# Where group 0's q and k are cut in two: strips 4 + 3 and 3 + 4, or 5 + 2 and 2 + 5

## The chip, the core and the metric

One NeuronCore of a Trainium2 chip runs the whole program. The metric is the device time of one execution in microseconds (us). The profile comes from one execution; its span is some 1.8 us shorter than the device time of the same execution (387.1 against 388.88 us for the kernel before). Engine names are those of the profile: PE is TensorE's matrix products, PEld its weight loads, DVE is VectorE, ACT is ScalarE, POOL is GpSimd, SP the sync engine. SP, ACT and POOL each issue DMA transfers from a queue of their own. "Group 0" is the first four heads of the first batch entry; a group has 7 strips of 64 tokens.

## The reference

Sigmoid attention over 8 batch entries, 12 heads, 448 tokens and head size 64, then a two-layer network with the tanh form of GELU over the 3584 tokens.

```python
scores = scale * np.matmul(q, k.transpose(0, 1, 3, 2)) - np.log(S)
attn = 1.0 / (1.0 + np.exp(-scores))
attn_out = np.matmul(attn, v)                     # (8, 12, 448, 64)
x = attn_out.transpose(0, 2, 1, 3).reshape(B * S, H * D)
h = x @ w_in                                      # 768 -> 2048
g = 0.5 * h * (1.0 + np.tanh(c * (h + 0.044715 * h * h * h)))
return g @ w_out                                  # 2048 -> 768
```

## The kernel before

The kernel plans itself at build time: operations with dependencies and modelled costs go into a list scheduler, which fixes the order of every engine. On the chip each engine then executes its list in that order and waits on semaphores.

Group 0 is special: its k and q are loaded, cast to bf16, transposed on TensorE and copied out of PSUM in two parts each, so that the first scores can start early.

```python
CUTS = {"q": ((0, NJ // 2 + 1), (NJ // 2 + 1, NJ)), "k": ((0, 3), (3, NJ))}     # NJ = 7: q 4 + 3, k 3 + 4
...
if g == 0:
    for x, (lo, hi) in enumerate(CUTS[nm]):
        both = [plan.add(Op("ld%s0.%d.%d" % (nm, x, c), eng, ... dma_start(d[:, c:c + w, lo * D:hi * D], ...),
                 ..., pkt=(8 * w, FIRST * (hi - lo) / NJ)))        # modelled packets
                for (eng, c, w) in (("AQ" if (nm, x) == ("q", 0) else "SP", 0, 2),)]
...
# group 1: q on ACT's queue after the warm-up activation, k on SP's
ld[g] = plan.add(Op(..., "AQ" if (nm, g) == ("q", 1) else "SP", ..., ([warm1] if (nm, g) == ("q", 1) else []) + ...))
...
# the first v load, on GpSimd's queue, waits for k's first part
deps = later(av, g - NVB) + (ld_k[(0, 0)].ops if g == 0 else [])
...
# part casts: modelled cost by strips; k's second part waits for the copy of q's second
who = "ACT" if (nm, x) == ("q", 1) else "DVE"
... (hi - lo) * (107.0 if who == "ACT" else 75.0) + 60.0, ...
...
def qk_needs(g, j):            # what a strip's scores wait for
    if g:
        return [tr_q.get(g), tr_k.get(g)]
    return [tr_q.get((0, 0)), tr_q.get((0, 1)), tr_k.get((0, 0 if j < CUTS["k"][0][1] else 1))]
...
plan.run()                     # fixes the orders
waits, level = emit(plan, None, None)
```

## Time and profile before

| | kernel before |
|---|---|
| device time, first three runs | 389.72 us median (389.63 to 389.81) |
| span of the profiled execution | 387.1 us |
| PE busy | 382.0 us (99%), from 40 to 380 us 339.95 of 340.00 |
| ACT | five sigmoids from 7.43 us, 0.23 us idle, sixteen from 11.82; second table load at 25.11 |
| chain that ended last | opens with the load of group 1's q, issued 2.81, landed 9.47 |

Read it from the end: TensorE has no room after some 30 us, so only the start can move the time, and in the start the question is which wait ends last. The prediction shows the lines.

### The profile page before, as it was taken

The page shows a single profiled execution, that of the slowest core. Times are in us where ns is not written, and L with a number is a line of the kernel's source. Part 1 is how long each engine was busy: PE and PEld are TensorE (multiplying, and loading weights), DVE is VectorE, ACT ScalarE, POOL GpSimd, SP SyncE. Part 2 cuts the span into 40 slices and gives each one's busy share as a digit, 9 for nine tenths or more (in the row PEclk, how much of TensorE's full clock was granted, in tenths as well). Part 3 has the DMA queues.
Part 4 walks back from the last instruction along what each step waited for, and adds up shares of the span by engine and source line. Part 5 has one row for each costly group of instructions (what it writes and reads, how often), then busy time and mean ns, then how long its engine had stood idle before and what let it go on. Part 6 is the DMA issues. An engine that isn't in the chain of part 4 may idle for free.

```text
span 387.1 us, 7517 instructions
## 1 busy us (share of the span) xinstructions
PE 382.0 (99%) x3218; PEld 203.7 (53%) x3218; DVE 155.8 (40%) x273; ACT 227.6 (59%) x337; POOL 53.1 (14%) x84
## 2 busy tenths in 40 slices
PE   8999999999999999999999999999999999999996
PEld 5434445555555555555555555554555555555565
DVE  3446733147680085702864057610767017400000
ACT  4999962268564575546755476635856467544221
POOL 5994110001110111001110011100201000000000
PEclk9999999999999999999999999999999999999999
DMA  8999999747885079903779048950779401110133
GB/s 226 186 203 203 209 206 321 121 88 182 186 194 103 8 171 210 233 5 109 147 204 204 4 120 203 204 99 0 185 185 215 82 0 42 43 41 2 41 83 81
DMA packets 64226, 51.74 MB, mean 134 GB/s; under 512 B 36289, under 2 KB 60737, under 8 KB 64193
## 3 DMA queue, kind: packets, MB, share of 16 engines
q1 hardware_dynamic: 48928, 36.81, 39.3%
q0 software_dynamic: 14560, 13.64, 22.4%
q10 hardware_dynamic: 704, 0.82, 0.6%
q8 instruction: 25, 0.41, 0.4%
q14 instruction: 9, 0.07, 0.0%
HBM read 45.61 MB, written 11.01 MB: 146 GB/s over the span
## 4 chain that ended last, share of the span: by engine, by line
PE 94%; ACT 3%; DMA 2%; DVE 1%; issue 0%; ACTq 0%
PE ps L824 39%; PE ps L779 36%; PE ps L632 9%; PE ps L680 7%; ACT at L643 2%; DMA qf<-in_q_dram 2%; PE ps L755 2%; PE ps L589 1%; ACT L377 0%; ACT th L652 0%; DVE qb L363 0%; DVE at L656 0%; DVE kb L363 0%; PE ps L586 0%; ACT xT L362 0%
## 5 line engine op out<-in xcount | busy, mean ns | idle before, releaser
L652 ACT ACTIVATE th<-ps 128x896 f32<-128x896 f32 x147 | 126.9, 928 | 45.2 <-PE ps L632 45.2
L824 PE MATMUL ps<-w_out,gT 128*128 128x384 bf16 (+2 forms) x912 | 152.9, 324 | 0.1
L779 PE MATMUL ps<-xT,w_in 128*128 128x448 bf16 x738 | 143.3, 353 | 0.0
L656 DVE TENSOR_SCALAR at<-th 128x896 bf16<-128x896 f32 x147 | 92.0, 626 | 127.3 <-ACT th L652 126.5
L824 PEld LDWEIGHTS ps<-w_out,gT 128*128 128x128 bf16 x912 | 85.9, 98 | 65.5 <-ACT th L652 5.9
L793 ACT ACTIVATE gT<-ps 128x448 bf16<-128x448 f32 x128 | 69.7, 549 | 79.2 <-PE ps L779 78.3
L779 PEld LDWEIGHTS ps<-xT,w_in 128*128 128x128 bf16 x738 | 71.4, 98 | 68.3 <-issue 3.1
L632 PE MATMUL ps<-qT,kT 64*64 64x448 bf16 x672 | 48.1, 358 | 0.3 <-ACT at L643 0.2
L512 POOL DMA_DIRECT2D vb<-in_v_dram x24 | 14.9, 620 | 237.7 <-PE ps L632 234.5
L680 PE MATMUL ps<-at,vb 64*64 64x448 bf16 x672 | 38.0, 350 | 0.1
L363 DVE COPY ob<-ps 128x384 f32<-128x384 f32 x43 | 23.9, 555 | 25.4 <-PE ps L824 24.3
L632 PEld LDWEIGHTS ps<-qT,kT 64*64 64x64 bf16 x672 | 15.7, 105 | 24.2 <-issue 9.8
L680 PEld LDWEIGHTS ps<-at,vb 64*64 64x64 bf16 x672 | 19.5, 107 | 12.1 <-issue 1.1
L362 ACT ACTIVATE ob<-ps 128x384 f32<-128x384 f32 (+2 forms) x14 | 6.6, 468 | 25.4 <-PE ps L824 25.4
L363 DVE CAST xT<-ps 128x448 bf16<-128x448 f32 x27 | 16.6, 623 | 11.0 <-PE ps L680 11.0
L514 POOL DMA_DIRECT2D vb<-in_v_dram x24 | 18.3, 762 | 0.2 <-issue 0.2
L643 ACT ACTIVATE at<-ps 128x896 bf16<-128x896 f32 x21 | 17.4, 924 | 0.7 <-PE ps L632 0.7
L363 DVE CAST kb<-kf 128x896 bf16<-128x896 f32 (+2 forms) x21 | 12.8, 610 | 11.0 <-DMA kf<-in_k_dram 10.5
L363 DVE CAST qb<-qf 128x896 bf16<-128x896 f32 (+1 forms) x20 | 12.3, 616 | 1.5 <-DMA qf<-in_q_dram 1.5
L362 ACT ACTIVATE xT<-ps 128x448 bf16<-128x448 f32 x21 | 11.6, 551 | 1.9 <-PE ps L680 1.9
L888 POOL DMA_DIRECT2D w_in<-in_moe_w_in_dram x16 | 10.2, 703 | 0.0
L436 PE MATMUL ps<-gT 128*128 128x128 bf16 (+1 forms) x54 | 6.9, 285 | 1.1 <-DVE gT L428 1.1
(31 smaller groups left out, 50.2 us busy)
## 6 DMA issues: line engine op xcount, KB each, us to landing
out_dram<-ob SPq DMA_DIRECT2D x54, 192.0 KB, 3.4
kf<-in_k_dram SPq DMA_DIRECT2D x19, 448.0 KB, 4.4
qf<-in_q_dram SPq DMA_DIRECT2D x18, 448.0 KB, 6.0
vb<-in_v_dram POOLq DMA_DIRECT2D x48, 112.0 KB, 5.4
w_out<-in_moe_w_out_dram POOLq DMA_DIRECT2D x4, 768.0 KB, 21.5
w_in<-in_moe_w_in_dram POOLq DMA_DIRECT2D x12, 192.0 KB, 11.6
kb<-in_k_dram POOLq DMA_DIRECT2D x4, 224.0 KB, 8.9
qb<-in_q_dram POOLq DMA_DIRECT2D x4, 224.0 KB, 9.3
```

Of the source, the lines that this page charges most:

```text
L362: return e.activation(o, i, AF.Copy)
L363: return e.tensor_copy(o, i)
L512: a = plan.add(Op("ldv%da" % g, "SWQ", lambda e, d=dst[0:64], ap=lo: e.dma_start(d, ap), deps, 610.0, 0.0, prio=order_v(g), sem="ldv%da" % ...
L514: c = plan.add(Op("ldv%db" % g, "SWQ", lambda e, d=dst[64:128], ap=hi: e.dma_start(d, ap), deps, 610.0, 0.0, prio=order_v(g), sem="ldv%db" ...
L632: r = mm(ps[64 * half:64 * half + 64, (x, y)[a], 0:S], kv[d, a, j, :], qv[d, a, :, :], start=True, stop=True)
L643: lambda e: e.activation(at[as_][:], both, AF.Sigmoid, bias=bias, scale=scale),
L652: lambda e: e.activation(th[ts][:], both, AF.Tanh, bias=0.5 * bias, scale=0.5 * scale),
L656: lambda e: e.tensor_scalar(at[as_][:], th[ts][:], 0.5, 0.5, op0=ALU.mult, op1=ALU.add),
L680: r = mm(ps[64 * c:64 * c + 64, banks[a], 0:S], vb[s][d, slot, j, :], at[as_][d, a, :], start=(j == 0), stop=(j == NJ - 1))
L779: r = mm(ps[:, bank, 0:S], w_in[:, kt, fc * 128:(fc + 1) * 128], xT[xb][:, kt, :], start=(kt == 0), stop=(kt == KT - 1))
L793: lambda e: e.activation(gT[:, fc, col:col + S], ps[:, bank, 0:S], AF.Gelu_apprx_tanh),
L824: r = mm(ps[:, bank, 0:hi - lo], gT[:, fc, col:col + 128], w_out[:, fc, lo:hi], start=(fc == 0), stop=(fc == FC - 1))
```

## The change

The intent: k's first part, on which the first scores wait, becomes smaller, so that 9 strips instead of 10 must land before the first scores. The price is a larger second part of k, on which the third strip's scores now wait too (before, only the fourth and later ones: `j < 3` above).

```diff
-        CUTS = {"q": ((0, NJ // 2 + 1), (NJ // 2 + 1, NJ)), "k": ((0, 3), (3, NJ))}
+        CUTS = {"q": ((0, 5), (5, NJ)), "k": ((0, 2), (2, NJ))}
```

This is the whole diff. The line reaches both the chip (sizes of loads, casts, transposes, copies) and the planner (their modelled costs).

## The prediction

> **What bounds the kernel now.** I read the page's busy shares first, then the chain that ended last in order of time, then the ACT timeline of the first 30 us, the waits there, and the DMA issues with their landing times. TensorE is busy 382.0 us of the 387.1 us span, and from 40 to 380 us it is busy 339.95 of 340.00 us. The change touches nothing there. It touches the first 9 us, so the question is how much later or earlier TensorE reaches its closed stretch. The chain tells what decides that:
>
> ```profile
> PE 382.0 (99%) x3218; PEld 203.7 (53%) x3218; DVE 155.8 (40%) x273; ACT 227.6 (59%) x337; POOL 53.1 (14%) x84
> ...
> 2.81 6.66 DMA qf<-in_q_dram
> 9.46 0.02 issue
> 9.48 0.76 DVE qb L363
> 10.24 0.60 DVE kb L363
> 10.85 0.04 issue
> 10.89 0.56 PE ps L586 x7
> 11.46 0.34 PE ps L632 x4
> 11.80 0.02 issue
> 11.82 3.35 ACT at L643 x4
> ```
>
> The columns are start, duration, engine and line. The transfer in the chain is 448 KB, issued at 2.81 us on ACT's queue: q of group 1, not of group 0. It lands at 9.47; VectorE casts q1, then k1 (k1 was issued at 2.26 and took 6.8, so it landed at 9.06 and waits for q1's cast in VectorE's fixed order); TensorE transposes k1, and only behind these seven transposes in its own fixed order come the scores of group 0's sixth strip, which start the sixth sigmoid at 11.82. From there ACT is closed:
>
> ```profile
> 7.43 4.15 ACT L643 ACTIVATE at<-ps 128x896 bf16<-128x896 f32 x5 [0.49 <-PE ps L632]
> 11.82 13.27 ACT L643 ACTIVATE at<-ps 128x896 bf16<-128x896 f32 x16 [0.23 <-PE ps L632]
> 25.11 1.28 ACT L648 ACT_TABLE_LOAD   x1
> ```
>
> Five sigmoids run from 7.43 to 11.58, ACT then idles 0.23 us, and sixteen run from 11.82 to 25.09 without a gap. All of group 0's own start (loads, casts, transposes, copies) lies before 7.43, its second part of k before 9. So group 0's path ends in **0.23 us of slack**.
>
> The loads concerned, with KB and us from issue to landing:
>
> ```profile
> kf<-in_k_dram SPq DMA_DIRECT2D x1, 448.0 KB, 6.8
> qf<-in_q_dram ACTq DMA_DIRECT2D x1, 448.0 KB, 6.7
> ...
> qf<-in_q_dram ACTq DMA_DIRECT2D x1, 256.0 KB, 4.0
> kf<-in_k_dram SPq DMA_DIRECT2D x1, 256.0 KB, 4.3
> kf<-in_k_dram SPq DMA_DIRECT2D x1, 192.0 KB, 3.6
> ...
> qf<-in_q_dram SPq DMA_DIRECT2D x1, 192.0 KB, 4.0
> ```
>
> A strip is 64 KB. With the issue times 0.74, 0.74, 1.26 and 1.75, the first part of k landed at 4.36, the first of q at 4.74, the second of q at 5.33 (ACT's cast starts there) and the second of k at 6.05.
>
> **What the Trainium skill says.** "DMA: Bandwidth & Descriptors", Issuing engines are not separate DMA queues: transfers issued from different engines run on the same 16 DMA engines and interleave. The trace agrees: in slices of 0.3 us from 3.0 to 5.4 us they move 346 to 392 GB/s, mean 371, at a busy digit of 9, though three queues issue. So what a load waits for is the bytes in front of it, whichever queue they are in. The same page, Specifications, puts the smallest transfer at full rate at 512 B; the new parts of two strips have rows of 2 x 64 x 4 = 512 B, just there, so I take no loss (no run yet shows it). "VectorE: DVE Perf Modes", The TRN2 errata: a fixed cost for each instruction plus cycles by size; at two elements a cycle and 0.96 GHz a strip of 128 elements adds 67 ns. The trace agrees: the cast of 384 columns took 360 ns, that of 512 took 427. "ScalarE: Activation LUTs", What ACT_TABLE_LOAD costs, gives one element a cycle at 1.2 GHz, 107 ns for a strip; the trace has ACT's cast of three strips at 523 ns and its copy at 491, and no second size to check the slope by.
>
> **The change part by part.** The number of instructions stays: two loads, two casts, two sets of transposes and two copies for q and for k, 14 transposes in all. Only sizes move.
>
> 1. Loads. Before the first score k's first part and all of q must land: 3 + 7 = 10 strips before, 2 + 7 = 9 after. One strip at 371 GB/s is 0.18 us, so q's second part should land near 5.15 instead of 5.33. The first parts of k and q together are seven strips in both kernels (3 + 4, 2 + 5), and so are the second parts; so q's first part, which is larger but shares with a smaller k, lands near 4.74 again, k's second part near 6.05, and q1 and k1 have the same bytes in front of them.
> 2. To the first score. VectorE casts q's five strips in 427 + 67 = 494 ns, from 4.76 to 5.25 (before: 5.19). TensorE starts q's transposes 0.17 us later, as before, 5.42; ACT's cast of two strips, 523 - 107 = 416 ns from 5.15, is done at 5.57, in time. Before, VectorE's copy of four strips began 0.77 us after the first of q's weight loads, ACT's of three strips 0.33 us after that, so 0.11 us for each transpose. After: VectorE's copy of five strips starts at 5.42 + 0.77 + 0.11 = 6.30 and takes 425 + 67 = 492 ns to 6.79; ACT's of two starts at 6.30 + 0.22 = 6.52 and takes 491 - 107 = 384 ns to 6.90. The old end was 6.95. So **the first score gains 0.05 us**, not the 0.18 us of the transfer, since the seven transposes start from VectorE's longer cast.
> 3. k's second part. Its cast waits for ACT's copy of q. The old path: cast 7.05 to 7.65 (600 ns), transposes, copy 8.14 to 8.56, third score at 8.54 (from the timeline). Five strips instead of four add about 0.08 (cast: 360 ns at three strips, 670 at seven, so 78 a strip) + 0.06 (a transpose; 7 took 0.56 - 0.16) + 0.07 (copy) = 0.21 us; less the 0.05 of step 2 the third score comes at 8.70. The third sigmoid started 9.04, some 0.43 after a score is enough, so 8.70 gives 9.13. **The third sigmoid is 0.09 us later than now.** It uses slack of 0.07 that was there and opens a hole of some 0.14 us against the second.
> 4. Groups 0's first five sigmoids thus end near 11.58 + 0.09 = 11.67. The sixth still waits for TensorE, 11.82. The slack falls from 0.23 to 0.14 us plus what the hole takes, and **nothing reaches the end**.
> 5. q1's landing. The v loads on GpSimd's queue wait for k's first part (wait of 3.2 us ended by kf). With two strips it may land 0.1 to 0.35 us sooner (nothing if the queues take turns row by row, two strips' worth of bytes if byte by byte: 128 KB at 371 GB/s). Then v enters the shared engines earlier and, with a third of them for 0.35 us, puts at most some 40 KB before q1: 0.1 us later. This part is on the path one for one. I take + 0.05.
>
> Sum: 0 from steps 1 to 4, + 0.05 from step 5: 389.72 + 0.05, say **389.8 us**.
>
> **The rivals.** (a) The early start reaches the end: if ACT were the chain from 7.43 on, the gain would be 0.05 to 0.18 us, 389.55 to 389.65. Against it speak the 0.23 us of idle and the chain, which passes through q1's load and not through group 0. (b) k's second part becomes the bound: the third score comes after its slot. If step 3 is short by 0.2 us, because VectorE's cast of five strips runs slower next to the descriptor writing of GpSimd (the cast of k's four strips took 600 ns, q's four 427), the hole exceeds the slack and 0.1 to 0.3 us reach the end: 389.8 to 390.0. (c) The order changes. The kernel's own planner at build time orders each engine's instructions by modelled times, in which the strip counts enter; shifted times can change the order of scores, transposes, first-layer parts and filler matmuls anywhere. For a small effect: the sums of strips are unchanged in each phase, so the planner's q1 and k1 hardly move, and the first score shifts by a little. For a large one: list scheduling at ties is jumpy. If k1's cast came ahead of q1's, it could start at 9.06 instead of 10.24, the sixth score would no longer wait and up to 0.23 us would be won, plus whatever follows. A bad reordering near 25 to 35 us, where ACT goes over to the other activation table and TensorE is not quite closed, could cost some tenths. A TensorE closed for 340 us leaves later orders little to lose: I give - 0.4 to + 0.8 us. (d) Row sizes of 512 B move slower than thought; both short parts are 256 KB in all, and even a halved rate costs 0.35 us in front of q1: 390.1.
>
> **Range and chances.** The three runs of before lie within 0.18 us. Steps 1 to 5 with (a), (b) and (d) cover 389.5 to 390.1; (c) widens it more to the slow side, since the old cut looks chosen by trial. I take 389.2 to 390.5. Two per cent are 7.8 us, which is more than everything before the first score can be worth (7.43 us of span), so: faster 0.01, same 0.98, slower 0.01.
>
> **What would show it.** In the changed profile the chain should still open with q of group 1 on ACT's queue, landing at 9.4 to 9.6 (step 5), with the sixth sigmoid near 11.8 to 11.9. The first sigmoid should start at 7.3 to 7.45 (step 2); ACT should show a small new hole before the third sigmoid (step 3); k's cast of 640 columns should take 0.65 to 0.7 us. The landings should be about 4.1 to 4.3, 4.7, 5.15 and 6.05 (step 1). I would be wrong if the chain went through group 0's load or through k's second part, if q1 landed away from 9.5 by more than 0.2 us, or if the order on VectorE around 9.5 to 11 us were another: then the reordering, and not the strips, made the time.

## The result

The changed kernel took 389.62 us (median of 6 runs, 389.31 to 390.03), the kernel before 389.53 us beside it (388.99 to 389.81). The ratio is 1.0005 with a 95% interval of 0.9992 to 1.0018: the same. A ratio here and below is the mean time of one kernel's fast runs over that of the other's of the same rounds, so not quite the ratio of the medians quoted.

All of the profile's totals stay: PE is busy 382.4 us of a span of 387.7. But the chain of waits does not open as before. From the chain that ended last of the changed kernel, in order of time (start, duration, engine and line):

```profile
8.27 0.50 DVE kT L363
8.77 0.04 issue
8.81 0.38 PE ps L632 x4
...
11.57 0.50 PE ps L586 x7
...
13.81 0.25 PE ps L632 x4
14.06 0.02 issue
14.08 9.84 ACT at L643 x12
```

And ACT's own timeline in the changed kernel (the idle time before, and who ended it, in brackets):

```profile
7.38 6.03 ACT L643 ACTIVATE at<-ps 128x896 bf16<-128x896 f32 x7 [0.55 <-PE ps L632]
14.08 11.45 ACT L643 ACTIVATE at<-ps 128x896 bf16<-128x896 f32 x14 [0.68 <-PE ps L632]
25.55 1.28 ACT L648 ACT_TABLE_LOAD   x1
```

The gap before the sixth sigmoid is gone; one of 0.68 us stands before the eighth, the first of group 1. The chain runs through group 0's second part of k and then through TensorE, where the profile strings filler products (L436, which only keep TensorE busy and whose results nobody reads) and scores together; the transposes of k1 (L586 at 11.57) now stand behind the sixth strip's scores and no longer before them. So **TensorE's order changed**. The table load, after which ACT turns to the tanh form, comes at 25.55 instead of 25.11 us.

The loads of the changed kernel (KB, us from issue to landing):

```profile
kf<-in_k_dram SPq DMA_DIRECT2D x1, 448.0 KB, 7.5
qf<-in_q_dram ACTq DMA_DIRECT2D x1, 448.0 KB, 7.4
...
qf<-in_q_dram ACTq DMA_DIRECT2D x1, 320.0 KB, 4.0
kf<-in_k_dram SPq DMA_DIRECT2D x1, 320.0 KB, 4.2
...
kf<-in_k_dram SPq DMA_DIRECT2D x1, 128.0 KB, 3.4
qf<-in_q_dram SPq DMA_DIRECT2D x1, 128.0 KB, 3.9
```

Group 0's parts land in this profile as predicted. But q1, issued at 2.80, took 7.4 us instead of 6.7: VectorE starts its cast at 10.20 instead of 9.48. Two profiles thus differ by 0.6 us of span, and in two things at once: the landing of q1 and the order. Which of them comes from the change?

### The profile page after: what moved, and what is told of

Its sections match the earlier page's. It is cut to its first block, busy times and chain, and to the rows that moved or that the text cites. A ratio compares the mean times of both kernels' runs of the same rounds, so it can differ in the third digit from the quotient of the medians.

```text
span 387.7 us, 7524 instructions
## 1 busy us (share of the span) xinstructions
PE 382.4 (99%) x3221; PEld 203.7 (53%) x3221; DVE 155.8 (40%) x273; ACT 227.4 (59%) x337; POOL 53.1 (14%) x84
## 4 chain that ended last, share of the span: by engine, by line
PE 94%; ACT 3%; DMA 1%; DVE 1%; issue 0%; DVEq 0%
PE ps L824 39%; PE ps L779 36%; PE ps L632 9%; PE ps L680 7%; ACT at L643 3%; PE ps L755 1%; DMA kf<-in_k_dram 1%; PE ps L586 1%; PE ps L436 1%; PE ps L589 0%; DVE kb L363 0%; ACT th L652 0%; DVE at L656 0%; ACT xT L362 0%; DVE kT L363 0%
## 5 line engine op out<-in xcount | busy, mean ns | idle before, releaser
L824 PE MATMUL ps<-w_out,gT 128*128 128x384 bf16 (+2 forms) x912 | 152.9, 324 | 0.1
L824 PEld LDWEIGHTS ps<-w_out,gT 128*128 128x128 bf16 x912 | 85.9, 98 | 65.5 <-ACT th L652 5.9
L436 PE MATMUL ps<-gT 128*128 128x128 bf16 (+1 forms) x57 | 7.3, 284 | 1.1 <-DVE gT L428 1.1
```

The costliest lines, as they stand in the source:

```text
L824: r = mm(ps[:, bank, 0:hi - lo], gT[:, fc, col:col + 128], w_out[:, fc, lo:hi], start=(fc == 0), stop=(fc == FC - 1))
```

## The experiments

All kernels below gave correct results. As the spans carry the argument, here they are together. "q1's cast" is when VectorE starts it, which in all but k1_first is set by q1's landing. Round 1 ran on chip 6, round 2 on chip 2 and round 3 on chip 15, so times are compared within a round; but the scatter is not one between chips alone: on chip 6 the unedited kernel's eleven runs have spans of 386.6 to 389.9 us. "First w_out product" is the start of the first product of the second layer (line L824 of the kernel before), read from PE's timeline.

| kernel | cut | order | q1's cast | table load | first w_out product | span |
|---|---|---|---|---|---|---|
| before | old | old | 9.48 | 25.11 | 60.31 | 387.1 |
| aa_before | old | old | 10.16 | 25.61 | 60.81 | 387.6 |
| sizes_only | new | old | 10.19 | 25.68 | 60.88 | 387.7 |
| late_q1 | old | old | 10.16 | 25.71 | 60.92 | 387.7 |
| v_later | old | old | 9.54 | 26.04 | 61.25 | 388.6 |
| k1_first | old | old, one swap | 10.49 | 24.66 | 59.87 | 387.3 |
| after | new | new | 10.20 | 25.55 | 60.91 | 387.7 |
| aa_after | new | new | 10.35 | 26.13 | 61.50 | 388.3 |
| order_only | old | new | 10.67 | 26.16 | 61.52 | 388.3 |
| late_q1_new | new | new | 8.93 | 24.82 | 60.18 | 386.9 |
| free_old | old | old, two swaps | 10.62 | 24.86 | 60.07 | 386.8 |
| free_sizes | new | old, two swaps | 10.16 | 25.05 | 60.25 | 387.0 |
| free_new | new | new, two swaps | 9.79 | 25.44 | 60.81 | 387.6 |

Two sums hold in it. From the table load to the first w_out product every kernel with the old order takes 35.20 or 35.21 us, every kernel with the new one 35.36 or 35.37. From there to the end it is 326.7 to 326.8 us, except in k1_first and v_later, 327.4. So in all but these two the span is the table load's time plus a constant, and **the start decides**.

### Round 1: sizes and order apart, and each kernel once more

The four kernels are a square: old and new sizes on the chip, with the old and the new order. In sizes_only the planner reckons with the old strips while loads, casts, transposes and copies use the new ones; its plan is the same as that of the kernel before, line for line. order_only is the converse. All were timed in 5 rounds.

aa_before and aa_after are the two kernels without an edit.

> The kernel before, unchanged, timed against itself: the noise floor and a second profile of it. Every theory: ratio 1.000 within 0.0015. If q of group 1 lands at 9.3 to 9.6 us again (first profile: 9.47) and the sixth sigmoid starts near 11.8, those times belong to the kernel; if q1's landing wanders by 0.5 us or more between profiles of one kernel, the 0.7 us by which it was later in the changed kernel's profile can be chance.

Measured: 389.15 us median, ratio 0.9988 (0.9966 to 1.001). From ACT's timeline of this second profile of the kernel before, and from its chain:

```profile
7.09 4.15 ACT L643 ACTIVATE at<-ps 128x896 bf16<-128x896 f32 x5 [0.49 <-PE ps L632]
12.32 13.27 ACT L643 ACTIVATE at<-ps 128x896 bf16<-128x896 f32 x16 [1.07 <-PE ps L632]
25.61 1.28 ACT L648 ACT_TABLE_LOAD   x1
```

```profile
2.81 7.34 DMA qf<-in_q_dram
```

The same program now has q1 landing at 10.15 instead of 9.47, a gap of 1.07 us instead of 0.23, and a span of 387.6 instead of 387.1. **The first profile of the kernel before was an early one** (its 388.88 us lie below all six timed runs, 388.99 to 389.81); most of the 0.6 us between the two first profiles is chance.

> The changed kernel once more. Theory A (order): the scores of group 0's sixth strip stand before k1's transposes in TensorE's order, so ACT runs seven sigmoids from 7.4 without a gap and idles 0.5 to 0.7 us before group 1's first one at 14.0 to 14.1, wherever q1 lands before 10.2. Theory B (q1's landing): the gap follows q1; if q1 lands at 9.5 this time, group 1's first sigmoid starts before 13.7. Time under both: ratio 1.000 to 1.002.

Measured: 389.89 us median, ratio 1.0004 (0.9981 to 1.0028). q1 was cast at 10.35, so the case of an early q1 did not arise and theories A and B were not told apart here. ACT's gaps are 0.56 us before the seventh sigmoid, 0.68 before the eighth and 0.31 before the fifteenth; seven sigmoids without a gap, as A had it, was wrong for this execution. The last gap is new: group 3's k, loaded on GpSimd's queue, landed at 19.35 and held up scores.

> New cuts on the chip, but the planner reckons with the old ones: every engine has the order of the kernel before (the plan is the same line for line). Theory A (order makes what difference there is): the sixth sigmoid waits for k1's transposes as before and ACT's gap stands there, 0.1 to 0.3 us if q1 lands near 9.5; span within 0.15 us of before, ratio 0.9995 to 1.0005. Theory B (sizes make q1 later through the earlier v loads): q1 lands at 10.0 to 10.3, the sixth sigmoid starts near 12.5, ACT's gap is 0.8 to 1.0 us, ratio about 1.0015 to 1.002.

```diff
-        CUTS = {"q": ((0, NJ // 2 + 1), (NJ // 2 + 1, NJ)), "k": ((0, 3), (3, NJ))}
+        CUTS = {"q": ((0, 5), (5, NJ)), "k": ((0, 2), (2, NJ))}
+        PCUTS = {"q": ((0, NJ // 2 + 1), (NJ // 2 + 1, NJ)), "k": ((0, 3), (3, NJ))}
+        # every modelled cost, the packet sizes and the planner's readiness test use PCUTS;
+        # the waits of the scores use CUTS
```

Measured: 389.63 us median, ratio 0.9993 (0.997 to 1.0017). The gap stands before the sixth sigmoid, as in the kernel before, with 1.04 us. q1 was cast at 10.19, which is what theory B expected; but aa_before has 10.16 with the old sizes, so it can be as late without the new sizes. Table load 25.68 against 25.61 in aa_before: **with equal landings of q1, old and new sizes give equal starts**.

> Old cuts on the chip, but the order of the changed kernel on every engine (third score made to wait for k's second part as there). Theory A: ACT runs seven sigmoids without a gap and idles 0.5 to 0.7 us before group 1's first near 14.0, although q1 lands near 9.5; span 0.3 to 0.6 us above before, ratio about 1.001. Theory B: q1 lands near 9.5 and the time is that of before or lower, ratio 0.999 to 1.000.

```diff
-        CUTS = {"q": ((0, NJ // 2 + 1), (NJ // 2 + 1, NJ)), "k": ((0, 3), (3, NJ))}
+        CUTS = {"q": ((0, NJ // 2 + 1), (NJ // 2 + 1, NJ)), "k": ((0, 3), (3, NJ))}
+        PCUTS = {"q": ((0, 5), (5, NJ)), "k": ((0, 2), (2, NJ))}
+        # costs, packets, readiness and the scores' waits by PCUTS
```

Measured: 389.49 us median, ratio 0.9995 (0.9971 to 1.0019). ACT's timeline:

```profile
7.67 4.97 ACT L647 ACTIVATE at<-ps 128x896 bf16<-128x896 f32 x6 [0.49 <-PE ps L636]
13.10 0.92 ACT L647 ACTIVATE at<-ps 128x896 bf16<-128x896 f32 x1 [0.46 <-PE ps L636]
14.69 11.45 ACT L647 ACTIVATE at<-ps 128x896 bf16<-128x896 f32 x14 [0.68 <-PE ps L636]
```

The gap of 0.68 us before the eighth sigmoid comes with the new order, on old sizes. But q1 landed still later here (cast at 10.67), and the span of 388.3 us goes with that. Neither theory in its pure form held: the order moves the gap, q1's landing sets how late it all is, and it wanders in both kernels.

### Round 2: is it q1's landing, and what can be done about it

The theory now was C: q1's landing carries the span, wanders from run to run, and the cut does not matter. Its rival D was GpSimd's queue (v, and k and q of groups 2 to 5). The edits are made after the plan is fixed, so that nothing else changes. Three rounds each.

```diff
         plan.run()
+        named("AQ", "ldq1").deps.append(ld_k[(0, 0)].ops[0])     # late_q1, and late_q1_new on the changed kernel
```

> The kernel before with one wait more: ACT issues q of group 1 only when k's first part has landed (issue near 4.4 us instead of 2.8), every order as before. Theory C (q1's landing carries the span, and it wanders from run to run; the cut does not matter): in the three profiles with the old order q1 landed at 9.47, 10.15 and 10.17 us and ACT's second table load came at 25.11, 25.61 and 25.68, some 0.7 us for each us, with the span 362.0 us after it. If q1 lands at 11.0 to 11.5 now, the table load comes at 26.2 to 26.8 and the span is 388.2 to 388.8. Rival D (v and k3 on GpSimd's queue carry it): table load stays at 25.5 to 25.7, span 387.5 to 387.7.

Measured: 389.60 us median, ratio 1.0002 (0.9978 to 1.0027). The experiment did not do what it was made for. From the loads of late_q1:

```profile
kf<-in_k_dram SPq DMA_DIRECT2D x1, 448.0 KB, 4.9
...
qf<-in_q_dram ACTq DMA_DIRECT2D x1, 448.0 KB, 5.8
```

q1 was issued at 4.37 instead of 2.81 and landed at 10.13 all the same, as in aa_before. k1, issued at 2.26, landed at 7.16 instead of 9.06: the two share the engines, and with q1 starting later k1 is finished first. As q1 did not move, neither did the span, which agrees with C but is no test of it.

> The same added wait in the changed kernel. Theory C: the same lateness; with the new order the spans so far are 362.15 us after the table load, so with q1 at 11.0 to 11.5 the table load comes at 26.2 to 27.0 and the span is 388.3 to 389.1; against the kernel before with the wait within 0.5 us. If the cut mattered once q1 is out of the way of chance, the two late kernels would differ by more than that.

Measured: 388.79 us median, ratio 0.9987 (0.9968 to 1.0006). Here q1, issued at 4.24, landed at 8.93, the earliest of all, and the table load came at 24.82: with the new order, from 26.13 (aa_after, of which 0.31 us are the wait for group 3's k) to 24.82 as q1's cast goes from 10.35 to 8.93. ACT's gap before the eighth sigmoid is still 0.65 us. It belongs to the order: q1's transposes stand behind the seventh strip's scores, and behind them four strips of attention-times-v (three in the old order). Those products start at 12.13 us, the copy of q1 on VectorE ends at 12.86, and group 1's first scores start at 12.92; which of the two holds them is not told apart. The two late kernels differ by more than the 0.5 us that the expectation allowed (medians 389.60 and 388.79 us, the changed kernel ahead). But their q1 landed 1.2 us apart in the profiles, where the expectation had reckoned with the same lateness in both, and the intervals overlap, so this says nothing of the cut.

> The kernel before with two neighbours on VectorE exchanged: k1 is cast before q1, all else in order. Theory C': the sixth sigmoid waits for k1's transposes only because k1's cast stands behind q1's. With k1 landing 0.4 us before q1 and its cast no longer behind, ACT's first gap (0.23 and 1.07 us in the two profiles of before) falls to 0 to 0.4 us; the table load comes at 24.8 to 25.2 even if q1 lands near 10.2, span 386.8 to 387.2. Rival D: the gap moves to about 20 us, where scores wait for k of group 3, and the table load stays at 25.4 to 25.7.

```diff
+        o = plan.order["DVE"]
+        x = [op.name for op in o].index("castq1")
+        o[x], o[x + 1] = o[x + 1], o[x]                  # castk1 ahead of castq1
```

Measured: 389.02 us median, ratio 0.999 (0.997 to 1.001). ACT's timeline of k1_first:

```profile
7.25 17.39 ACT L643 ACTIVATE at<-ps 128x896 bf16<-128x896 f32 x21 [0.58 <-PE ps L632]
24.66 1.28 ACT L648 ACT_TABLE_LOAD   x1
```

All 21 sigmoids run without a gap, though q1 landed at about 10.5. This is the direct test of the first link of the chain: **the sixth sigmoid waited for q1 only because k1's cast stood behind q1's**. The table load came 0.95 us ahead of aa_before's. Of that, 0.6 us were lost again. Two lines from the later timelines of k1_first, one of VectorE, one of PE:

```profile
67.95 0.63 DVE L363 CAST kb<-kf 128x896 bf16<-128x896 f32 x1 [0.54 <-DMA kf<-in_k_dram]
69.10 1.31 PE L779 MATMUL ps<-xT,w_in 128*128 128x448 bf16 x6 [0.40 <-DVE ob L363]
```

The loads of groups 6 to 8 wait until w_out has landed (some 57 us). VectorE casts group 8's k before it evacuates (copies out of PSUM, the memory that TensorE writes) the second half of the first output rows; when that load lands late, the evacuation is late, a PSUM bank is not free, and TensorE stands. A second carrier lies close behind the first. The profile marks 0.40 of the 0.6 us as idle. v_later, though its TensorE was late and not early, stands at the same place (0.44 us before 70.45) and loses the same.

> The kernel before with GpSimd's first v load also waiting for q's second part (about 5.2 us instead of 4.4), orders as before. If the v, k and q loads on GpSimd's queue are what stretches q1's tail, q1 lands at 8.8 to 9.5 us and the sixth sigmoid starts near 11.4 to 11.8. Theory C alone: table load 24.9 to 25.2. Rival D: everything on GpSimd's queue is 0.8 us later, k of group 3 lands near 20 and scores wait for it, a new gap of 0.3 to 0.8 us near 20 us, table load 25.3 to 25.8. If q1 still lands near 10.2, the load on GpSimd's queue is not its cause.

```diff
+        named("SWQ", "ldv0a").deps.append(ld_q[(0, 1)].ops[0])   # v waits for q's second part too
```

Measured: 389.57 us median, ratio 1.0006 (0.9983 to 1.0029). q1 was cast at 9.54, inside the scatter of the kernel before (9.48 and 10.16), so whether GpSimd's loads stretch q1's tail stays open. A gap of 0.65 us opened before 17.58, where attention-times-v had waited 0.81 us; the profile names no releaser, but v comes by the queue that was made later. The span was the longest of all, 388.6. So rival D has its place too, one step behind, but with a wait earlier than the one near 20 us that it foretold.

### Round 3: q1 off the path, for each cut and order

Three edits together: q1 issued after k's first part (k1 lands first), k1 cast before q1, and on VectorE the evacuation of the first output rows before the cast of group 8's k.

```diff
+        named("AQ", "ldq1").deps.append(ld_k[(0, 0)].ops[0])
+        o = plan.order["DVE"]
+        x = [op.name for op in o].index("castq1")
+        o[x], o[x + 1] = o[x + 1], o[x]
+        x = [op.name for op in o].index("castk8")
+        o[x], o[x + 1] = o[x + 1], o[x]                  # evo0.1 ahead of castk8
```

They were put on the kernel before (free_old), on sizes_only (free_sizes) and on the changed kernel (free_new); 5 rounds, beside the same 11 runs of the kernel before (median 389.46 us).

> The kernel before with q1 taken off the path: q1 issued when k's first part has landed (as in late_q1, where k1 landed at 7.2 us), k1 cast before q1 (as in k1_first), and, against the stall of 0.4 us at 69 us that k1_first showed, the evacuation of the first output rows put before the cast of group 8's k on VectorE. Theory C: 21 sigmoids without a gap, table load at 24.4 to 24.8 us, the first second-layer product at 59.6 to 60.0 (24.66 and 59.87 in k1_first), no stall after it, span 326.8 us later: 386.4 to 386.8. Time 388.0 to 388.7, ratio 0.996 to 0.9985. If the ratio is above 0.9995 the front does not carry the time.

Measured: 388.50 us median, ratio 0.9977 (0.9965 to 0.9989), an interval clear of 1 though only a quarter of one per cent. The 21 sigmoids run from 7.33 without a gap that the timeline marks; q1's cast at 10.62 is the second latest of all and costs nothing. No stall follows at 69 us. **With q1 off the path the span is the shortest measured**, so theory C holds for the kernel before.

> The same three edits on sizes_only, so the new cuts with the old order: now the first sigmoid and the third carry the time, and the cut is alone on the path. By the prediction's steps 2 and 3 the first sigmoid starts 0.05 us sooner and the third opens a hole of some 0.1 us: table load within 0.15 us of free_old's, later rather than sooner, ratio to free_old within 0.0005. Rival: the cut is worth its 0.18 us of transfer (table load 0.15 us or more ahead of free_old's) and was only hidden by q1.

Measured: 388.72 us median, ratio 0.9984 (0.9971 to 0.9997). The sigmoids again run without a marked gap, from 7.51; the hole before the third did not appear. The table load is 0.19 us behind free_old's, and the first sigmoid is 0.18 us behind it, which is inside the scatter (with the old cut the first sigmoid starts at 7.09 to 7.67 us in seven profiles, with the new at 6.93 to 7.51 in six). But the cut was not alone on the path. The chain that ended last in free_old no longer passes through the first sigmoids; it goes from k's first part through GpSimd's queue to a load of w_in:

```profile
0.74 3.67 DMA kf<-in_k_dram
...
9.53 6.82 DMA w_in<-in_moe_w_in_dram
16.35 0.14 issue
16.48 0.54 PE ps L755 x2
```

In free_sizes it is the same chain, and the load lands at 16.53, 0.18 us later. So a further path lies right behind q1, and whether it or the first sigmoid makes the 0.19 us is not told apart. The cut by itself shows no gain and no loss beyond the scatter.

> The same three edits on the changed kernel, so the new cuts with the new order. Theory C: in the new order the scores of group 1's first strip stand behind four strips of attention-times-v on TensorE, so ACT keeps a gap of 0.6 to 0.7 us before the eighth sigmoid whatever q1 does (0.65 in late_q1_new with q1 at 8.9 us); table load 24.8 to 25.3, 0.3 to 0.6 us behind free_old, span 386.9 to 387.4. Rival: the order costs nothing, table load as free_old's.

Measured: 389.32 us median, ratio 0.9993 (0.998 to 1.0006). ACT's timeline:

```profile
6.96 5.78 ACT L643 ACTIVATE at<-ps 128x896 bf16<-128x896 f32 x7 [0.58 <-PE ps L632]
13.38 5.78 ACT L643 ACTIVATE at<-ps 128x896 bf16<-128x896 f32 x7 [0.65 <-PE ps L632]
19.65 5.78 ACT L643 ACTIVATE at<-ps 128x896 bf16<-128x896 f32 x7 [0.49 <-PE ps L632]
25.44 1.28 ACT L648 ACT_TABLE_LOAD   x1
```

The first sigmoid is 0.37 us earlier than in free_old, yet the table load is 0.58 us later: the new order's gap of 0.65 us stays, and a second of 0.49 us waits for k of group 3, as in aa_after. That k's transposes stand before group 2's first scores here (18.70 and 19.21 us) and behind them in free_old (18.86 and 18.36). The mean of free_new's five runs is 389.27 us, that of free_old's 388.62: **0.66 us from the same three edits, but on another order and another cut**. Against free_sizes, which has the same cut (mean 388.87 us, one of six runs at 390.13), it is 0.40 us, and the two intervals overlap. So the gaps show that the order costs something when q1 does not hide it; how much, the times do not settle.

## Why the prediction was right, and where not

The time was right: 389.62 us against 389.8, within 389.2 to 390.5. Its central statement, that group 0's own path ends in slack made by q1's load, is what the experiments show for the kernel before: sizes_only equals aa_before, and free_old gains by taking q1 off. Luck has a part in the number: the unedited kernel alone took 388.42 to 391.72 us in eleven runs, so a forecast of no change was hard to miss. And two of the prediction's own signs of being wrong came, the chain through k's second part and q1 more than 0.2 us away from 9.5. So the hit does not confirm the steps:

- **Step 1, the loads.** The landings in the changed profile are those foretold (4.19, 4.76, 5.17 and 5.96 us, by the starts of the casts, or issue and landing, against 4.1 to 4.3, 4.7, 5.15 and 6.05). But the gain of 0.18 us for q's second part is not in the repeats: ACT's cast of it starts at 5.16 to 5.40 us in seven profiles with the old cut, mean 5.26, and at 5.14 to 5.59 in six with the new, mean 5.27. The first profile of before, with 5.33, was one draw. Nor did k's first part, a third smaller, land sooner: its cast starts at 4.30 us on average with either cut (4.18 to 4.43 in the seven, 4.18 to 4.59 in the six). What the change was made for is not seen.
- **Step 2, to the first score.** Right in each term in the first profile: VectorE's cast 0.49 us, its copy 0.49, ACT's cast 0.42, its copy 0.38 (so the 107 ns a strip, for which the prediction had no second size, hold); first sigmoid 7.38 as worked out. Over all profiles the mean start is 7.31 us with the old cut and 7.19 with the new, with a scatter of 0.6 us in each, so a gain of 0.05 us cannot be seen in it.
- **Step 3, k's second part.** Its starting point was misread. In the kernel before the third strip belongs to k's first part, and its scores started at 8.54 us, just before the copy of the second part ended (8.56). The step takes the one for the result of the other; the wait is new with the changed cut (copy to 8.76, scores at 8.81). That the two times fell together made the sum come out near, 8.70 against 8.81. The cast of 640 columns took 0.78 us in the first profile of the changed kernel, more than the 0.68 worked out, and the third sigmoid started at 9.24, not 9.13. In the five other profiles with the new cut it took 0.49 to 0.56 us and there was no hole. So the term was a chance value of 0.60 us in the kernel before, carried on; with the old cut the same cast takes 0.43 us in five profiles and 0.60 and 0.61 in two (before and v_later). The Trainium skill, "SBUF — State Buffer", Who interferes with whom, says that casts on VectorE can contend with GpSimd for a shared pair of ports, whole instruction against whole instruction; here GpSimd was issuing loads from 6.67 to 8.00 us, beside the cast from 6.94 to 7.72. That fits, but GpSimd was issuing loads beside the casts of 0.43 us too. Those five lay within one issue; in the two of 0.60 and 0.61 us the next issue began during the cast. It began so in all six with the new cut, which spread from 0.49 to 0.78 us. No run here tested it.
- **Step 4, the sixth sigmoid.** This is the step that failed. It took for granted that TensorE's order stays. In the new order the sixth strip's scores come before k1's transposes, and the gap before the sixth sigmoid is gone. In its place ACT waits 0.65 to 0.68 us before the eighth sigmoid in all five profiles with the new order, and 0.46 and 0.56 before the seventh in the two with the latest q1. Rival (c), reordering, came true; its size had been put at - 0.4 to + 0.8 us. The measured size stays open. From the table load to the first w_out product the new order takes 0.16 us more (35.36 against 35.20). At nearly equal q1 the table load came at 25.55 (after), against 25.61 to 25.71 with the old order (aa_before, late_q1, sizes_only), so the two nearly cancel: the first w_out product at 60.91, against 60.81 to 60.92. But aa_after, with q1 some 0.2 us later, is 0.6 us behind these. The measured ratio of 1.0005 (0.9992 to 1.0018, so - 0.3 to + 0.7 us) cannot resolve it.
- **Step 5, q1's landing.** Foretold 0.05 us later; seen 0.7 us later in the first pair of profiles. No effect of the change is shown by that: aa_before has it at 10.15 too. The earlier v that the step rests on did not come either: GpSimd issued its first v load at 4.64 and 4.46 us in the two profiles of the kernel before, at 4.49 and 4.63 in those of the changed one. The mistake was to read a landing from one profile as a constant of the kernel. The slack of 0.23 us, on which steps 3 and 4 rest, was as much a draw: 1.07 us in the repeat.

Rival (a) did not occur. Of (b) a part did: in the first profile of the changed kernel the third sigmoid came 0.20 us later than in the kernel before (9.24 against 9.04), and the chain passes through k's second part. But k1's cast ended there at 11.43 and k1's transposes began at 11.50, so q1 alone would have held TensorE nearly as long; the other profiles with the new cut have no hole. The large form of rival (d) was not seen: the 128 KB parts landed in 3.4 and 3.9 us. Whether the short rows ate the small gain of step 1 is not shown; no run changed the rows alone.

What stays open is why q1's landing wanders between 8.9 and 10.7 us. Issued 1.56 us later it landed no later in late_q1, and issued 1.43 us later it landed earliest of all in late_q1_new; delaying v by one wait left it inside the scatter.

## What to carry to other kernels

Before a fraction of a microsecond in one profile is explained, profile the unchanged kernel a second time; here it differed from itself by 0.5 us of span, nearly the 0.6 us between the first profiles of the two kernels. Where a parameter feeds both the hardware and a scheduler that fixes orders, test the two apart: freeze the order and change the sizes, then the reverse. And where an engine works through a fixed order, a late transfer costs what stands behind its first user, so put the user of the earlier-landing transfer first. Here k1 before q1 brought the table load forward by 0.95 us in the profile, where the cut of the loads ahead brought nothing that the runs show; in device time it was clear of noise only together with the two other edits of free_old.

## What the Trainium skill lacked or had wrong

- "DMA: Bandwidth & Descriptors" rightly says that queues share the engines and interleave. It does not say how far one load's landing then wanders: the same 448 KB, issued at 2.8 us, was ready for its cast between 9.48 and 10.67 us in eight profiles (k1_first, whose cast stood behind another, lies inside).
- The same page has nothing on staggering two loads of one size. With q1 issued 1.56 us later, k1 landed 1.9 us sooner (7.16 instead of 9.06 us) and q1 at 10.13, no later than in the repeat of the kernel before (10.15).
- "VectorE: DVE Perf Modes", The TRN2 errata, gives a time by size alone. The same cast of 128 x 640 values took 0.49 to 0.78 us in six profiles, that of 128 x 512 (k's second part) 0.43 in five and 0.60 and 0.61 in two. "SBUF — State Buffer" names a possible reason; no run here isolates it.
- No page that I read says that one profile is one draw; between two profiles of one program the span moved by 0.5 us, with equal constants of 35.20 and 326.8 us behind a start that wandered.
